# One load of a streaming add is issued in two parts, the second in short rows

## The chip, the cores and the metric

The kernel runs on one core of one Trainium2 chip. The metric is the device time of one execution in microseconds; the figure for a kernel is the median of its runs. A profile of one execution gives a span, from its first to its last instruction.

## The reference

```python
B, S, D = 512, 32, 640        # x, fx: bf16 [512, 32, 640]; alpha: bf16 [1]
def reference(x, fx, alpha):
    return x + alpha * fx
```

Each of the three large tensors holds 10,485,760 bf16 numbers, 20.97 MB. Two of them are read and one is written, so 62.91 MB pass through the core, with one multiplication and one addition for each number.

## The kernel before

The tensors are viewed as 128 partitions with 80 units in each. A unit is K = 1024 numbers, 2048 bytes, and the units of one partition lie next to each other in memory, so a piece of n units is 128 rows of n x 2048 bytes in a DMA.

`x` is cut into three pieces, X = units 0-32, 32-64 and 64-80, which are called x0, x1 and x2 here. `fx` is cut into five, FX = units 0-16, 16-32, 32-51, 51-67 and 67-80, called f0 to f4. The pools `wide` (for x) and `fs` (for fx) have two buffers each. So x2 takes the buffer of x0 and has to wait until the store of x0 has left it; f2 takes the buffer of f0 and waits for the computation on f0; f3 takes that of f1, and f4 that of f2.

The order is written out by hand in PLAN, which is carried out step by step; the scheduler moves nothing. In short:

```
x 0, a, f 0, f 1, x 1, c 0 0, f 2, c 1 0, s 0, f 3, x 2, c 2 1, f 4, c 3 1, c 3 2, s 1, c 4 2, s 2
```

- `x i` (load_x, line 77) and `f j` (load_f, line 85) load a piece, `s i` (store, line 104) stores one. All of them are DMAs that SP issues, in this order, on one hardware queue. x0 is issued as two DMAs, 4 units and 28 units (X_CUTS); every other piece is one DMA.
- `a` (alpha_to_lanes, line 109) loads alpha and spreads it over the 128 partitions with one small matmul; the result lands in `a_f`.
- `c j i` (compute, line 92) is one VectorE instruction, `x_t = f_t * a_f + x_t`, over the units that f_j and x_i share. It writes in place, and the store reads the x tile. f3 straddles x1 and x2 and has two of these (`c 3 1`, 13 units, and `c 3 2`, 3 units).

SP stands at an issue whose condition is not met yet, and everything behind it in the list waits too. Stores wait for VectorE, loads into a used buffer wait for VectorE or, for x2, for the store of x0. At the end SP waits for all that is under way (line 126).

Each DMA of 128 rows is spread over the core's 16 DMA engines, 8 rows to an engine: the trace holds 1730 packets, of which 1536 are rows (12 large DMAs x 128), and the rest are completions of 4 bytes and the one element of alpha. An engine works off its rows in the order of issue.

Of the kernel before, what the change touches and what calls it, by code (L numbers as in the profile page):

```python
# [2 lines left out]

# [4 lines left out]

ACT = mybir.ActivationFunctionType
ALU = mybir.AluOpType  # L10
F32 = mybir.dt.float32
BF16 = mybir.dt.bfloat16

K = 1024
P = 128


X = [(0, 32), (32, 64), (64, 80)]
FX = [(0, 16), (16, 32), (32, 51), (51, 67), (67, 80)]

X_CUTS = {0: (4,)}
PLAN = """
x 0
a
f 0
f 1
x 1
c 0 0
f 2
c 1 0  # L30
s 0
f 3
x 2
c 2 1
f 4
c 3 1
c 3 2
s 1
c 4 2
s 2  # L40
"""


@with_exitstack
def kernel(
    ctx: ExitStack,
    tc: tile.TileContext,
    x: bass.AP,
    fx: bass.AP,
    alpha: bass.AP,  # L50
    out: bass.AP,
):

    nc = tc.nc
    xv = x.flatten_outer_dims().rearrange("(p n) d -> p (n d)", p=P)
    fxv = fx.flatten_outer_dims().rearrange("(p n) d -> p (n d)", p=P)  # L60
    ov = out.flatten_outer_dims().rearrange("(p n) d -> p (n d)", p=P)
    assert xv.shape[1] == X[-1][1] * K == FX[-1][1] * K

    consts = ctx.enter_context(tc.tile_pool(name="consts", bufs=1))
    psum = ctx.enter_context(tc.tile_pool(name="psum", bufs=1, space=bass.MemoryType.PSUM))
    wide = ctx.enter_context(tc.tile_pool(name="wide", bufs=2))
    fs = ctx.enter_context(tc.tile_pool(name="fs", bufs=2))
    ctx.enter_context(tc.manual_schedule())

    xt, ft = {}, {}  # L70
    done = []

    def load_x(i):
        a, b = X[i]
        xt[i] = wide.tile([P, max(e - s for s, e in X) * K], x.dtype, tag="x", name="x_t")
        for c, d in pairwise((a, *X_CUTS.get(i, ()), b)):
            r = nc.sync.dma_start(  # L77
                out=xt[i][:, (c - a) * K : (d - a) * K], in_=xv[:, c * K : d * K]
            )
            done.append(r)  # L80

    def load_f(j):
        a, b = FX[j]
        ft[j] = fs.tile([P, max(e - s for s, e in FX) * K], fx.dtype, tag="f", name="f_t")
        r = nc.sync.dma_start(out=ft[j][:, : (b - a) * K], in_=fxv[:, a * K : b * K])
        done.append(r)

    def compute(j, i):
        (fa, fb), (xa, xb) = FX[j], X[i]
        a, b = max(fa, xa), min(fb, xb)  # L90
        piece = xt[i][:, (a - xa) * K : (b - xa) * K]
        r = nc.vector.scalar_tensor_tensor(  # L92
            out=piece,
            in0=ft[j][:, (a - fa) * K : (b - fa) * K],
            scalar=lanes["a_f"][:],
            in1=piece,
            op0=ALU.mult,
            op1=ALU.add,
        )
        done.append(r)  # L100

    def store(i):
        a, b = X[i]
        r = nc.sync.dma_start(out=ov[:, a * K : b * K], in_=xt[i][:, : (b - a) * K])
        done.append(r)

    lanes = {}

    def alpha_to_lanes():
        a_1 = consts.tile([1, 1], alpha.dtype, name="a_1")  # L110
        done.append(nc.sync.dma_start(out=a_1[:], in_=alpha[None, :]))  # L111
        ones = consts.tile([1, P], alpha.dtype, name="ones")
        nc.vector.memset(ones[:], 1.0)  # L113
        a_ps = psum.tile([P, 1], F32, name="a_ps")
        done.append(nc.tensor.matmul(a_ps[:], ones[:], a_1[:], start=True, stop=True))  # L115
        lanes["a_f"] = consts.tile([P, 1], F32, name="a_f")
        nc.vector.tensor_copy(out=lanes["a_f"][:], in_=a_ps[:])  # L117

    does = {"x": load_x, "f": load_f, "c": compute, "s": store, "a": alpha_to_lanes}
    for step in PLAN.split("\n"):  # L120
        if step:
            what, *of = step.split()
            does[what](*map(int, of))


    rest = nc.sync.nop(nofuse=True)
    info = mybir.DependencyInfo(mybir.DependencyClass.Sync, mybir.DependencyReason.DATA)
    for i in done[:-1]:
        tc.add_manual_dep(rest.ins, i.ins.name, info, reason="all but the last store")


# [1 line left out]
_INS = ['x', 'fx', 'alpha']  # L133
_OUTS = [((512, 32, 640), 'bfloat16')]


# [23 lines left out]
```

## Time and profile before

| | |
|---|---|
| median of 3 runs | 152.03 us (151.96 to 152.31) |
| span of the profiled execution | 150.2 us |
| median less span | 1.8 us |
| VectorE (DVE) busy | 86.8 us, 58% of the span |
| DMA queue: share of 16 engines | 98.1% |
| bytes moved | 62.92 MB, mean 419 GB/s |
| packets | 1730, of them 194 under 512 bytes |
| instructions | 78 |

The page times the profiled execution by its span alone; what lies ahead of the first instruction and behind the last one is not on it. The 1.8 us above are the difference between the median of the timed runs and that span, and they are taken as the same for both kernels.

Times are in microseconds from the start of the span. "DMA share" is the mean busy share of the 16 engines. In a window, a packet counts with all its bytes and its whole time in the window in which it starts; so a share can be above 1, and GB/s can be trusted only where the window's ends fall on the ends of rows. In the chain of waits, "DMA" is the time between the issue of a transfer and the moment its waiter is released.

### The profile page before, as it was taken

The numbers are of one execution on the slowest core, as the hardware profiler recorded it, in microseconds if no ns is written. First come the engines' busy times: TensorE is split into PE (matmuls) and PEld (weight loads), VectorE is DVE, ScalarE is ACT, GpSimd is POOL, SyncE is SP. The second block draws the span as 40 slices with busy tenths as digits, with TensorE's granted clock in tenths as the row PEclk, the third lists the DMA queues.
The fourth block names the chain that finished last, engine by engine and source line by source line (L and its number), as shares of the span: only waits on it lengthen the run. The fifth ranks groups of instructions, "written<-read, shape, count | busy, mean of one in ns | idle before, by whom it ended". The sixth has DMA issues, their size and how long they took to land.

```text
span 150.2 us, 78 instructions
## 1 busy us (share of the span) xinstructions
PE 0.2 (0%) x1; PEld 0.1 (0%) x1; DVE 86.8 (58%) x8; POOL 0.2 (0%) x4
## 2 busy tenths in 40 slices
PE   0000000000000000000000000000000000000000
PEld 0000000000000000000000000000000000000000
DVE  0000000049999999970399999106999999980000
POOL 0000000000000000000000000000000000000000
DMA  5997989999969696999696999999999969696994
GB/s 179 589 428 305 489 384 419 436 454 471 576 297 559 279 559 279 497 394 435 279 559 279 559 401 410 445 419 419 419 393 454 620 279 559 279 559 297 454 463 183
DMA packets 1730, 62.92 MB, mean 419 GB/s; under 512 B 194, under 2 KB 194, under 8 KB 194
## 3 DMA queue, kind: packets, MB, share of 16 engines
q1 hardware_dynamic: 1730, 62.92, 98.1%
HBM read 41.94 MB, written 20.97 MB: 419 GB/s over the span
## 4 chain that ended last, share of the span: by engine, by line
DMA 54%; DVE 35%; SPq 1%; issue 0%; DVEq 0%
DMA f_t<-in_fx_dram 54%; DVE x_t L92 35%; SPq L77 1%; SPq L111 0%; DVEq L92 0%
## 5 line engine op out<-in xcount | busy, mean ns | idle before, releaser
L92 DVE SCALAR_TENSOR_TENSOR x_t<-f_t,a_f,x_t 128x16384 bf16<-128x16384 bf16 (+3 forms) x6 | 86.5, 14438 | 25.5 <-DMA f_t<-in_fx_dram 25.5
L117 DVE COPY a_f<-a_ps 128x1 f32<-128x1 f32 x1 | 0.2, 159 | 21.5 <-PE a_ps L115 21.5
L113 DVE MEMSET ones<- 1x128 bf16 x1 | 0.2, 165 | 0.8 <-PEq L144 0.8
L115 PE MATMUL a_ps<-a,ones 1*128 1x1 bf16 x1 | 0.2, 158 | 22.2 <-DMA a<-in_alpha_dram 22.2
L144 POOL MEMSET const-bfloat16-1.0<- 128x1 bf16 x1 | 0.1, 103 | 0.0
L144 POOL MEMSET const-uint8-127<- 128x1 uint8 x1 | 0.1, 103 | 0.0
L115 PEld LDWEIGHTS <-ones 1*128 1x128 bf16 x1 | 0.1, 100 | 1.0 <-DVE ones L113 1.0
L144 POOL MEMSET const-float32-1.0<- 128x1 f32 x1 | 0.1, 100 | 0.0
L144 POOL MEMSET const-float32-0.0<- 128x1 f32 x1 | 0.1, 99 | 0.2 <-issue 0.2
## 6 DMA issues: line engine op xcount, KB each, us to landing
f_t<-in_fx_dram SPq DMA_DIRECT2D x3, 4096.0 KB, 35.6
x_t<-in_x_dram SPq DMA_DIRECT2D x1, 7168.0 KB, 21.3
f_t<-in_fx_dram SPq DMA_DIRECT2D x1, 4864.0 KB, 24.1
x_t<-in_x_dram SPq DMA_DIRECT2D x1, 4096.0 KB, 19.2
out_dram<-x_t SPq DMA_DIRECT2D x1, 4096.0 KB, 14.9
f_t<-in_fx_dram SPq DMA_DIRECT2D x1, 3328.0 KB
x_t<-in_x_dram SPq DMA_DIRECT2D x1, 1024.0 KB, 4.8
out_dram<-x_t SPq DMA_DIRECT2D x2, 24.7
```

The costliest lines, as they stand in the source:

```text
L77: r = nc.sync.dma_start(out=xt[i][:, (c - a) * K : (d - a) * K], in_=xv[:, c * K : d * K])
L92: r = nc.vector.scalar_tensor_tensor(out=piece, in0=ft[j][:, (a - fa) * K : (b - fa) * K], scalar=lanes["a_f"][:], in1=piece, op0=ALU.mult ...
L113: nc.vector.memset(ones[:], 1.0)
L115: done.append(nc.tensor.matmul(a_ps[:], ones[:], a_1[:], start=True, stop=True))
L117: nc.vector.tensor_copy(out=lanes["a_f"][:], in_=a_ps[:])
L144: nc = _bacc.Bacc("TRN2", target_bir_lowering=False, num_devices=1)
```

## The change

The third fx piece, f2 (units 32 to 51), is loaded by two DMAs rather than one. The first takes units 32 to 49, 17 units, in one row of 34,816 bytes per partition as before. The second takes units 49 to 51 and is issued with rows of at most 1024 bytes: each partition's 4096 bytes go as 4 rows, 512 rows in all, 32 to an engine. Both are issued on SP at the place of the old one. The instruction `c 2 1` waits for both.

The diff also brings in two other tables, S_CUTS and AFTER, which are empty: stores stay whole, no step gets another condition. The other DMAs keep their shapes.

```diff
+RUN = 1024
+F_CUTS = {2: (49,)}
+S_CUTS = {}
+AFTER = {}
...
     def load_f(j):
         a, b = FX[j]
         ft[j] = fs.tile([P, max(e - s for s, e in FX) * K], fx.dtype, tag="f", name="f_t")
-        r = nc.sync.dma_start(out=ft[j][:, : (b - a) * K], in_=fxv[:, a * K : b * K])
-        done.append(r)
+        for c, d in pairwise((a, *F_CUTS.get(j, ()), b)):
+            r = nc.sync.dma_start(
+                out=ft[j][:, (c - a) * K : (d - a) * K],
+                in_=fxv[:, c * K : d * K],
+                max_dma_last_dim=RUN if c > a else 65536,
+            )
+            after(r, "f", j)
+            done.append(r)
+            parts["f", j, d] = r
...
     def store(i):
         a, b = X[i]
-        r = nc.sync.dma_start(out=ov[:, a * K : b * K], in_=xt[i][:, : (b - a) * K])
-        done.append(r)
+        for c, d in pairwise((a, *S_CUTS.get(i, ()), b)):
+            r = nc.sync.dma_start(
+                out=ov[:, c * K : d * K], in_=xt[i][:, (c - a) * K : (d - a) * K]
+            )
```

In the instruction lists of the two kernels SP has one row more, a DMA of 128x4x512 numbers behind one of 128x17408 where there was one of 128x19456. VectorE, TensorE and GpSimd have the same instructions in the same order.

## The prediction

> **What bounds the kernel.** I read the page first: which resource is full?
>
> ```profile
> PE 0.2 (0%) x1; PEld 0.1 (0%) x1; DVE 86.8 (58%) x8; POOL 0.2 (0%) x4
> ...
> q1 hardware_dynamic: 1730, 62.92, 98.1%
> ```
>
> VectorE works for 86.8 of 150.2 us; the DMA engines are busy for 98.1% of the span. So the end is set by 62.92 MB going through 16 engines, provided that the one queue never runs dry. The chain of waits names transfers and VectorE in turn, which could mislead, so I held SP's issues (the timeline) against the landings:
>
> ```profile
> 2.90 0.45 SPq L77 DMA_DIRECT2D x_t<-in_x_dram  x1
> 49.59 0.33 SPq L85 DMA_DIRECT2D f_t<-in_fx_dram  x1
> 66.78 0.35 SPq L104 DMA_DIRECT2D out_dram<-x_t  x1
> 67.19 0.42 SPq L85 DMA_DIRECT2D f_t<-in_fx_dram  x1
> 73.80 20.48 DVE L92 SCALAR_TENSOR_TENSOR x_t<-f_t,a_f,x_t 128x19456 bf16<-128x19456 bf16 x1 [7.04 <-DMA f_t<-in_fx_dram]
> 93.37 0.33 SPq L77 DMA_DIRECT2D x_t<-in_x_dram  x1
> 94.31 0.33 SPq L85 DMA_DIRECT2D f_t<-in_fx_dram  x1
> 116.95 17.96 SPq L104 DMA_DIRECT2D out_dram<-x_t  x2
> ```
>
> Every issue comes before the queue is empty. x1 lands 58.3 us after its issue at 2.90, at 61.2; f2 was issued at 49.59, 11.6 us ahead of that. f2 lands at 73.7; s0 and f3 were issued 6.9 and 6.5 us ahead. f3 lands at 102.8 (35.6 us after issue); x2 and f4 were there 9.4 and 8.5 us earlier. f4 lands at 120.4 and s1 was issued 3.5 us ahead; s2 was issued at 134.6, about 5 us ahead of the end of s1. VectorE's waits are therefore waits for the same queue, and the whole kernel moves as one with the time that the engines take per row.
>
> So the question is where the engines run below their pace. With windows whose ends fall on row ends (columns: window, its length, the engines' busy times, clock, DMA share, GB/s):
>
> ```profile
> 60.20:68.84 8.64, 0.00 (x0) 0.00 (x0) 6.56 (x1) 0.00 (x0) 1.00 1.00 432
> 68.84:72.98 4.14, 0.00 (x0) 0.00 (x0) 0.00 (x0) 0.00 (x0) 1.00 1.00 301
> 72.98:92.30 19.32, 0.00 (x0) 0.00 (x0) 18.50 (x1) 0.00 (x0) 1.00 1.00 434
> 111.65:119.54 7.89, 0.00 (x0) 0.00 (x0) 7.89 (x2) 0.00 (x0) 1.00 1.00 432
> ```
>
> The first two are f2: six rows of each engine at 432 GB/s, then the last two at 301. The third is s0, at 434 at once. The fourth is the whole of f4, which also has a store behind it, at 432 to its end. The DMA view of the slow window says the same by packets: 32 packets, two for each engine, and the engines are never free in it.
>
> ```profile
> DMA packets 32, 1.25 MB, mean 301 GB/s; under 512 B 0, under 2 KB 0, under 8 KB 0
> ...
> q1 hardware_dynamic: 32, 1.25, 100.4%
> ```
>
> The packet records of the trace put sizes to it. A row of 38,912 bytes takes 1439 to 1448 ns in rows 1 to 6 of f2, about 1.6 us in row 7 and about 2.5 us in row 8, on all 16 engines; the excess is 1.28 us per engine. Outside of f2 only the first rows of the kernel show one (0.5 us, the 8192-byte rows at the start, 392 to 876 ns where 309 is usual). The slow rows are the ones at which s0 (issued 66.78) already stands behind f2; the change puts short rows exactly there.
>
> **What the change costs.** Rows first. Usual durations by size are 309 ns (8192 B), 987 (26,624), 1213 (32,768), 1439 (38,912), 2116 (57,344) and 2418 (65,536): a straight line of 36.78 ns per 1000 bytes plus 7.7 ns, and each row starts 3 ns before the last one ends, so a row costs 4.7 ns beyond its bytes. An engine's 8 long rows lose 4096 bytes each, and 32 rows of 1024 bytes come in: 32 x 4.7 = 0.15 us, and one more completion packet of 9 ns, overlapped by 3. Sum **+0.16 us** on every engine, on the path. No large row here is below 8192 bytes, so 4.7 ns is the line continued; below, a row cannot cost less than nothing (0 us), and above I bound it by the excess that the 8192-byte rows had in their slow start, 83 ns at least: 32 x 83 = 2.7 us. I take the line, since six sizes lie on it and the start has ended by 3.3 us.
>
> The other edits. SP issues one more DMA, 0.3 to 0.5 us by its other issues, at 49.9; its next step is s0 at 66.78, held by VectorE, so 16 us cover it, and without that cover s0 would still be 6 us early. The queue gets one more completion; `c 2 1` waits for one more semaphore, a few hundredths by the chain's own steps (0.02 to 0.05 us), and what is behind it, f4's issue at 94.3, is 8.5 us early. These go at nothing.
>
> One rule speaks against the cut; this row comes first: four DMAs stand behind one another between 2 and 61 us, and x1 of 65,536-byte rows follows f1 without a gap. The Trainium skill ("DMA: Bandwidth & Descriptors", Anatomy of one DMA, and Rules for kernel authors) gives each DMA about 2.0 us fixed, measured on the GpSimd path, and asks for 1 MiB or more; the new part has 0.5 MB. By that the sum would be 2 us worse, 154.0. The trace shows back-to-back DMAs of this queue at 432 to 434 GB/s, so I leave it at zero.
>
> **What the change may bring.** Most to gain is the 1.28 us. The engine that was last when x1 ended (row end at 60.78) lost 1.1 us of it and is last at f2's end too (73.41); the last engine counts, so without the slow stretch f2 lands about **1.1 us** earlier. With +0.16 that is -0.98. What the slow stretch depends on is not in the trace. Two readings:
>
> Reading by rows: an engine takes up the next rows in its list before the current one is through, and when those belong to a store, the load's rows share the engine with it. Row 7 (0.2) and row 8 (1.07) are the two before s0. If it looks ahead by a few rows, few short rows are hit, a few kilobytes rather than 50. For it: the loss begins when the store is two rows off, and load behind load has none. f4 escaping fits if s1 (issued 116.95, some 2.6 us ahead of the first s1 row at 119.55) came too late to be taken up beside f4's rows. Reading by bytes: the stretch is the last 50 KB or so (row 8 and a third of row 7), whatever the rows are. Then nothing is won.
>
> A row that bears on this: f4's slowest engine ends its last row at 119.99 and the load is seen to have landed at 120.44, 0.45 us; at 27.2 bytes per ns, 12 KB are under way. Against it the Trainium skill ("HBM Reference", Latency) has 2 us for an access under high load; an estimate from that page is 54 KB under way, close to the stretch, which would speak for bytes and for a time of 152.2. I go with the row: 12 KB under way do not explain 50 slow KB, so it is not a matter of bytes alone.
>
> I take the reading by rows as the likeliest and let a fifth of a microsecond of the stretch remain (as row 7 kept 0.2 of it when the store was one row further off): -1.1 + 0.2 + 0.16 = -0.77, taken as -0.8 us. Span 150.2 - 0.8 = 149.4; with the 1.8 us around it, 152.03 - 0.8 = **151.2 us**. After f2 everything moves forward together: `c 2 1` starts at about 73.0, x2 and f4 are issued 0.8 earlier, s1 at about 116.1, 3.5 us ahead of f4's landing as before. Next late is still the queue.
>
> **The rivals.** (1) The stretch stays as long as it was: by bytes, or tied to the time since s0's issue, or an accident of this one execution that the median doesn't hold. Then only the rows count: 152.03 + 0.16 = 152.2 us. For it: one profile; f4 with no loss shows that a store behind a load is not enough. Against it: all 16 engines have it, and only there.
> (2) Slower: in the stretch the delay is paid per row, and there are 32 rows in place of one. For it: the start of the kernel, where 8192-byte rows, the shortest here, lost 83 to 567 ns each, while the 57,344-byte rows after them lost almost none. Against it: the start's rows recover within 2 us, with the same sizes. The balance lies where 32 short rows lose what the stretch lost less the 0.16: (1.28 - 0.16) / 32 = 35 ns per row, a row of 77 ns in place of 42. At 60 ns per row it is 1.9 + 0.16 - 1.28 = +0.8, 152.8 us; at 83 ns +1.5, 153.6.
> (3) The change does not do what it says: the rows might be joined again into long ones. The instruction list shows 128x4x512, so I give it no chance of its own; it would give 152.0.
>
> **How the numbers follow.** Forecast (stretch mostly gone, 150.9 to 151.6) 0.45; rival 1 (152.0 to 152.5) 0.27; rival 2 (152.4 to 153.6) 0.28. A measurement of this kernel can tell about 0.2%, 0.3 us, from no change. Rival 1 lies within that in 0.20 of its 0.27 and above it in 0.07. Faster 0.45, same 0.20, slower 0.07 + 0.28 = 0.35. The range must hold 8 in 10: from 150.9, all of the stretch gone with the row costs at zero, up through rival 1 and a third of rival 2, to 152.7. The forecast's own range is 150.9 to 151.6.
>
> **What would show it.** Right: the packets are 1730 + 512 rows + 16 = 2258; f2 lands near 72.9, the window of its last rows is above 400 GB/s, and short rows take 42 to 50 ns. s0 runs at 434 again. Wrong, by rival 1: f2 lands at 73.8, and the slow part now holds the short rows and the last long row, together still 1.2 us too long. Wrong, by rival 2: short rows above 77 ns and f2 landing after 74. Wrong in the ground: a gap in the queue in front of s0 or s1, or VectorE waiting for something else than the queue.

## The result and the profile after

The changed kernel took 152.30 us (median of 20 runs, 152.02 to 152.75) against 152.07 us for the kernel before (20 runs). The ratio is 1.0015, 95% interval 1.0009 to 1.0021: 0.23 us slower (0.14 to 0.32). The prediction was 151.2 us and faster; the figure of its first rival was 152.2. In a later comparison (e15 below) the same kernel stood at 0.9998 (0.9988 to 1.0008), no difference. So the change brought nothing; the 0.23 us were not seen a second time.

The lines of the page (span 150.4 us) that answer to those of before:

```profile
PE 0.2 (0%) x1; PEld 0.1 (0%) x1; DVE 86.8 (58%) x8; POOL 0.2 (0%) x4
...
q1 hardware_dynamic: 2258, 62.92, 98.0%
```

The packets are the 2258 of the prediction, and the kernel is bound as before. SP's issues and VectorE's wait for f2, from the timeline:

```profile
49.38 0.81 SPq L97 DMA_DIRECT2D f_t<-in_fx_dram  x2
66.57 0.35 SPq L123 DMA_DIRECT2D out_dram<-x_t  x1
66.97 0.43 SPq L97 DMA_DIRECT2D f_t<-in_fx_dram  x1
74.05 20.48 DVE L110 SCALAR_TENSOR_TENSOR x_t<-f_t,a_f,x_t 128x19456 bf16<-128x19456 bf16 x1 [7.51 <-DMA f_t<-in_fx_dram]
```

`c 2 1` starts at 74.05, where 73.0 was forecast and 73.80 was measured before. f2 did not come earlier. The windows show why; a row counts in the window in which it starts. The first has the first seven long rows of each engine and five of the sixteen eighth ones, the second the other eleven and 409 of the 512 short rows, the third the rest of the short rows and s0:

```profile
60.18:69.33 9.15, 0.00 (x0) 0.00 (x0) 6.36 (x1) 0.00 (x0) 1.00 1.05 445
69.33:73.00 3.67, 0.00 (x0) 0.00 (x0) 0.00 (x0) 0.00 (x0) 1.00 0.81 218
73.00:92.30 19.30, 0.00 (x0) 0.00 (x0) 18.25 (x1) 0.00 (x0) 1.00 1.02 440
```

At the usual pace one long row (1285 ns) and 32 short ones (42.4 ns) take 2.64 us. By the packet records an engine needed 3.90 us on average from the start of its eighth long row to the start of its first row of s0. The slow stretch is still there, in the same 3 to 4 us ahead of s0. The packet records show its make: of the 512 short rows 425 took 48 ns or less, 81 took more than 60, up to 451. So the short rows are not all slowed alike: most go at their usual pace, some are held up.

Below, "excess" is the time per engine that f2's rows (of whatever length) took beyond the line of the prediction, 36.78 ns per 1000 bytes plus 7.7 ns; it comes from the packet records of each run's one profile. It was 1.30 us before and 1.13 us after. Where rows are short it counts too little, because the engines also stand between two rows. From the first row of f2 to the first row of s0, on average over the engines, the load took 12.79 us before and 12.92 us after; that is 1.29 and 1.27 us beyond the usual pace of the rows. So the stretch lost as much as before, and the 0.13 us between the two loads is nearly the price of the short rows.

### The profile page after: what moved, and what is told of

Its sections match the earlier page's. It is cut to its first block, busy times and chain, and to the rows that moved or that the text cites. A ratio compares the mean times of both kernels' runs of the same rounds, so it can differ in the third digit from the quotient of the medians.

```text
span 150.4 us, 80 instructions
## 1 busy us (share of the span) xinstructions
PE 0.2 (0%) x1; PEld 0.1 (0%) x1; DVE 86.8 (58%) x8; POOL 0.2 (0%) x4
## 2 busy tenths in 40 slices
DMA packets 2258, 62.92 MB, mean 418 GB/s; under 512 B 210, under 2 KB 722, under 8 KB 722
## 3 DMA queue, kind: packets, MB, share of 16 engines
q1 hardware_dynamic: 2258, 62.92, 98.0%
## 4 chain that ended last, share of the span: by engine, by line
DMA 53%; DVE 34%; SPq 1%; issue 0%; DVEq 0%
DMA f_t<-in_fx_dram 53%; DVE x_t L110 34%; SPq L88 1%; SPq L97 0%; SPq L135 0%; DVEq L110 0%
```

## Experiments

All ratios are to the kernel before, on the same chip. All edits are made to the changed kernel's code, whose tables stand at `RUN = 1024`, `F_CUTS = {2: (49,)}`, `AFTER = {}`; AFTER names a DMA that is issued only when another has landed. The edits are shown in short. A letter such as R or S is a theory that the expectation of the run names.

**The cut without the short rows** (e1).

```diff
-RUN = 1024
+RUN = 65536
```

> f2 is cut at unit 49 as in the changed kernel, but the second part keeps long rows (128 rows of 4096 bytes, 8 to an engine). Theory S (a store that already stands in the queue slows the last 3 us or so of the load in front of it, whatever its rows are): the stretch stays at about 1.1 to 1.3 us per engine, and only 8 rows of 4.7 ns and one completion come in: +0.05 us on the kernel before, 152.1. Theory P (the loss belongs to the place or the moment, f2's own last bytes): the same. Theory R (the added time of the changed kernel comes from the split and the second semaphore, not from the short rows): 152.3, as the changed kernel.

151.86 us, ratio 0.9996 (0.9987 to 1.0006), excess 0.79 us. One more DMA, one more semaphore and 8 rows of 4096 bytes per engine cost nothing that can be measured. R, by which the cut itself costs the time, falls.

**The store moved behind f3** (e2).

```diff
-F_CUTS = {2: (49,)}
+F_CUTS = {}
-f 2, c 1 0, s 0, f 3, x 2, c 2 1, f 4, c 3 1
+f 2, c 1 0, f 3, s 0, c 2 1, f 4, x 2, c 3 1
```

> The kernel before with f3 issued ahead of s0, and f4 ahead of x2, so that f2 is followed by a load and f3 by the store; s1 is issued as soon as c 3 1 is done, which is some 10 us before x2 has landed. Theory S: f2's last rows go at 1439 to 1448 ns, the last 2 rows of f3 lose 1.1 to 1.3 us per engine instead, and x2's last rows lose as much again, because s1 now stands behind x2 long ahead: two stretches, about 153.2 us. Theory P: f2's last two rows lose 1.28 us as before and f3 and x2 lose nothing, 152.1.

152.04 us, 0.9999 (0.9988 to 1.0009). Windows: all of f2, then f3's first six rows per engine, then its last two, which are in front of s0 now.

```profile
60.40:71.93 11.53, 0.00 (x0) 0.00 (x0) 6.40 (x1) 0.00 (x0) 1.00 1.01 435
71.93:79.15 7.22, 0.00 (x0) 0.00 (x0) 6.27 (x1) 0.00 (x0) 1.00 1.00 431
79.15:82.30 3.15, 0.00 (x0) 0.00 (x0) 3.15 (x1) 0.00 (x0) 1.00 1.01 333
```

The stretch went with the store: f2 is clean (longest row 1449 ns), f3's end is slow, by 0.77 us. VectorE works all through it here and was idle in it before, so it has no part in it. P, by which the loss belongs to f2's own last bytes, falls. But S had a second stretch in front of s1, and there was none: x2's rows had no excess, although s1 was issued 12 us before they ended.

**s0 later, in three steps** (e3, e16 and e9).

```diff
-RUN = 1024
+RUN = 65536
-F_CUTS = {2: (49,)}
+F_CUTS = {2: (45,)}                      # e16: 42, e9: 46
-AFTER = {}
+AFTER = {("s", 0): ("f", 2, 45)}         # e16: 42, e9: 46
```

> f2 is cut at unit 45 with long rows in both parts, and s0 is issued only when the first part has landed, some 3 us before the second part has. Theory S: the store is not there yet while the engines take up f2's last bytes, as it is with s1 behind f4, and the loss is gone: f2's rows all at the pace of 36.78 ns per 1000 bytes, about 1.1 us less the row costs, 151.0 us. Theory P: f2's end loses 1.1 to 1.3 us all the same, 152.1. If s0 comes too late, a gap of some tenths shows ahead of its first row.

> f2 cut at unit 42 with long rows, s0 issued when the first part has landed, some 5.5 us before f2's end, between the 4.1 us (loss 0.37) and the 6.9 us (0.8 to 1.3) already seen. If the loss grows with the time that the store has stood in the queue: 0.5 to 0.9 us per engine, time 0 to 0.2 us under the kernel before. If there is a step at a fixed lead of 3 to 4 us, the full 0.8 to 1.3 us. If any wait of s0 for a part of f2 helps, whatever the lead: 0.1 us or less, 151.5.

> As the run in which s0 waits for the first part of f2, but cut at unit 46, so that s0 is issued some 3 us before f2's end rather than 4; s1 behind f4, with 3.5 us and no loss, lies between. If the loss depends on how long the store has stood in the queue: f2's rows lose 0.0 to 0.2 us per engine where that run had 0.34 and the kernel before 1.28, and the time is 0.5 to 0.9 us under the kernel before, 151.1 to 151.5. If that run's smaller loss was chance: 0.3 to 1.3 us again, 151.5 to 152.0.

| s0 issued ahead of f2's landing | excess at f2 | us | ratio |
|---|---|---|---|
| 6.2 us (e16) | 0.81 us | 151.98 | 0.9997 (0.9987 to 1.0006) |
| 4.1 us (e3) | 0.38 us | 151.67 | 0.9978 (0.9968 to 0.9989) |
| 3.0 us (e9) | 0.06 us | 151.53 | 0.9965 (0.9952 to 0.9977) |

The issue of s0 and the start of `c 2 1`, just after f2's landing, in e16 and then in e9:

```profile
67.56 0.35 SPq L123 DMA_DIRECT2D out_dram<-x_t  x1
73.85 20.48 DVE L110 SCALAR_TENSOR_TENSOR x_t<-f_t,a_f,x_t 128x19456 bf16<-128x19456 bf16 x1 [6.95 <-DMA f_t<-in_fx_dram]
```

```profile
69.94 0.35 SPq L123 DMA_DIRECT2D out_dram<-x_t  x1
73.08 20.48 DVE L110 SCALAR_TENSOR_TENSOR x_t<-f_t,a_f,x_t 128x19456 bf16<-128x19456 bf16 x1 [6.20 <-DMA f_t<-in_fx_dram]
```

The windows of e9, f2's first eight rows per engine, its second part, and s0:

```profile
60.25:68.78 8.53, 0.00 (x0) 0.00 (x0) 6.63 (x1) 0.00 (x0) 1.00 1.00 430
68.78:71.87 3.09, 0.00 (x0) 0.00 (x0) 0.00 (x0) 0.00 (x0) 1.00 0.95 398
71.87:91.20 19.33, 0.00 (x0) 0.00 (x0) 18.12 (x1) 0.00 (x0) 1.00 1.02 438
```

The second window ends with the first start of s0, so the last rows of the engines behind count in the third; the row records are sharper: none of e9's 10,240-byte rows took more than 396 ns, where the line gives 384. No gap stands ahead of s0. This version is faster than the kernel before by 0.53 us (0.35 to 0.73), and a store that comes late enough leaves the load alone. Not all of the loss is won: s0's own last rows, in front of f3, lost 0.16 us per engine in e9 and 0.13 us in e3, where they lost nothing in the kernel before and in e16.

**f3 issued late** (e4) and **s0 issued when f2 has landed** (e12).

```diff
-F_CUTS = {2: (49,)}
+F_CUTS = {}
+AFTER = {("f", 3): ("f", 2, 51)}         # e12: ("s", 0): ("f", 2, 51)
```

> The kernel before, only that f3 is issued when f2 has landed, so that s0 stands alone behind f2. Theory F (what slows f2's end is the load behind the store, which the engines take up at the same time): the loss is gone, 151.0. Theories S and P: f2's last two rows lose 1.1 to 1.3 us as before, 152.1; f3 is then still issued 19 us ahead of its turn.

> s0 is issued only when f2 has landed, so that nothing stands behind f2. If it takes a store in the queue to make the loss: f2's rows are clean, f2 lands at about 72.5; then the queue is empty until s0's first row, by the start of the kernel about 1.0 us from issue to first row plus 0.45 us of landing, so 151.97 - 0.9 + 1.5 = 152.6. If the loss is there without any store behind: 153.5.

e4: 151.92 us, 0.9996 (0.9987 to 1.0005), excess 0.81: a load behind the store is not what does it; F, which said so, falls. e12: 153.90 us, 1.0124 (1.0110 to 1.0138), excess 0.03; f2's last two rows:

```profile
69.00:71.95 2.95, 0.00 (x0) 0.00 (x0) 0.00 (x0) 0.00 (x0) 1.00 0.98 422
```

With no store in the queue there is no stretch. The time is 1.3 us above what was expected: the engines stood 1.7 us on average between f2's rows and s0's (from 73.85), and another 0.77 us went where it was not looked for, in s0's own last rows from 90.8 us on (up to 3533 ns where 2418 is usual), in front of f3. f4's end lost 0.2. A store in front of a load can be slowed too.

**Which store** (e5, e7, e11, e8).

```diff
 # all four: f2 uncut
-F_CUTS = {2: (49,)}
+F_CUTS = {}
 # e5, e7: unit 0 of x0 stored by itself right after c 0 0; in e7 on ScalarE's queue
+S_CUTS = {0: (1,)}
+c 0 0, s 0 (first part), f 2, c 1 0, s 0 (rest), f 3
 # e11: units 0 to 2 stored right behind f2
+S_CUTS = {0: (2,)}
 # e8: all of s0 on ScalarE's queue
+r = nc.scalar.dma_start(...)
```

> The kernel before, with unit 0 of x0 stored by a DMA of its own (128 rows of 2048 bytes) as soon as c 0 0 is done, ahead of f2, and the other 31 units at the old place. Theory W (the first store of an execution slows the load in front of it, whichever store that is): the loss moves to the last rows of x1, which is now in front of the first store, at 0.8 to 1.3 us per engine; f2's rows are clean; the time stays within 0.1 us of the kernel before. Theory Z (the loss belongs to the store of x0's 64-KB rows): x1's rows are clean and f2's last two rows lose 0.8 to 1.3 us as before.

> As the run with the small first store of unit 0, but this store is issued on ScalarE's queue, so that the loads on SP's queue do not stand behind or in front of it. Theory W, where the loss is a wait inside one queue: it is paid beside the loads, f2's last rows are clean, x1's too, 151.1. Theory W, where the loss falls on whatever the engines carry at that moment: some rows of x1 lose 0.8 to 1.3 us at about 50 to 53 us, f2's are clean, 152.0. Theory Z: f2's last two rows lose as before, 152.0.

> s0 is cut at unit 2: its first two units (128 rows of 4096 bytes) are issued right behind f2, 23 us before f2's end, and the other 30 at the old time. If the loss grows with the time that a store has stood behind the load: f2's end loses at least as much as in the kernel before, 0.8 to 1.3 us or more, 152.0. If it depends on the size of the store's rows that the engines have next (64 KB in the kernel before, 4 KB here): f2's end loses a few tenths at most, 151.2 to 151.5.

> The kernel before with s0 issued on ScalarE's queue: its rows alternate with the loads from about 68 us on, and no load stands in front of it in its queue. A wait inside one queue (W or Z): no rows lose, 151.1, if SP's queue never runs dry (f2 lands later, at about 80, c 2 1 ends at about 100, f4 is issued then, while f3 and s0 still run). A loss that falls on whatever the engines carry: rows near 69 to 72 us lose 0.8 to 1.3 us, 152.0.

e5: 151.75 us, 0.9984 (0.9975 to 0.9994); x1's last row lost 0.17 us and f2 still 0.54: the loss did not move from f2 to the load in front of the first store, so W, by which the first store does it, falls as it was put. Z expected 0.8 to 1.3 us at f2 and nothing at x1, and does not fit this run either. e7: 151.94 us, 0.9995 (0.9986 to 1.0004); excess at f2 1.08 us although a store had run before, and x1's rows lost nothing. e11: 151.89 us, 0.9995 (0.9986 to 1.0004), about 0.7 us at f2 with rows of 4096 bytes behind it and 23 us of lead: small rows in the store did not take it away, and more lead did not raise it. e8: 154.75 us, 1.0186 (1.0164 to 1.0207): rows lost time where the two queues ran beside each other (0.8 us at 69) and in front of s1 (1.0 us at 119 to 122), and the engines stood all but still around 102 to 103.5, because x2 and f4 were issued only at 102.7 and 103.1, after s0 had landed, when f3 was all but through.

**The price of the rows** (e6, e10, e17, e18, e13).

```diff
-F_CUTS = {2: (49,)}
+F_CUTS = {1: (24,)}     # e6: 128 short rows per engine in f1
+F_CUTS = {1: (30,)}     # e10: 32 in f1; e17: the same cut, RUN = 65536
+F_CUTS = {0: (14,)}     # e18: 32 in f0
+F_CUTS = {2: (46, 49)}  # e13: short rows from 49 on; AFTER = {("s", 0): ("f", 2, 46)}
```

> f2 is whole again; instead the second half of f1 (units 24 to 32, 16,384 bytes per partition) goes in rows of 1024 bytes, 128 to an engine, with no store anywhere near. By the line through the row durations of the kernel before, 4.7 ns for each row: 0.60 us, 152.0 + 0.6 = 152.5. By the rate at which the changed kernel lost against the kernel before (0.23 us for 32 rows, 7.2 ns each, were the slow stretch the same in both): 0.92 us, 152.9. If the short rows cost nothing away from a store: 152.0.

> The same 512 short rows of 1024 bytes, 32 to an engine, as in the changed kernel, but as the end of f1 (units 30 to 32), where a load follows. Row price: the 128 short rows of the earlier run took 46 to 60 ns, 9.3 ns on average beyond their bytes; 32 of these are 0.30 us, or 0.15 us by the line of the large rows. If the short rows alone make the changed kernel slower, this one is 0.15 to 0.30 us slower too, 152.15 to 152.3, and f2's end keeps its loss of 0.8 to 1.3 us. If short rows anywhere ahead of f2 shift the engines against each other so that the loss goes (as it had gone in the run with 128 of them): f2 clean, 0.5 to 0.9 us faster, 151.2 to 151.5.

> f1 cut at unit 30 with long rows in both parts, the control for the run with 32 short rows per engine at the same place, which was 0.23 us faster with 0.29 us lost at f2's end. If the short rows did that (by shifting the engines against each other ahead of f2), this run has the usual 0.7 to 1.3 us at f2's end and the time of the kernel before, 152.0. If the cut, or one more DMA in the queue, did it: 0.3 us at f2's end, 151.75.

> The same 512 short rows as the end of f0 (units 14 to 16), another place with no store near. If short rows ahead of f2 lessen the loss at its end: 0 to 0.4 us there, row price 0.15 to 0.3 us, time 0.1 to 0.4 us under the kernel before. If the run with f1 was chance: 0.7 to 1.3 us at f2's end, and the row price is all that is left, 152.15 to 152.3.

> f2 in three parts: units 32 to 46 and 46 to 49 in long rows, 49 to 51 in the changed kernel's 512 short rows; s0 is issued when the first part has landed, some 3 us before f2's end. The price of the short rows without the slow stretch: if it is what the other runs show (46 to 50 ns a row, 0.15 to 0.25 us in all, with 8 rows and one completion more for the third part, 0.05 us), the time is 0.2 to 0.3 us above the run with the cut at 46 alone, that is 0.2 to 0.3 us below the kernel before. If short rows cost more when a store follows, it is at or above the kernel before. If the late store doesn't take the loss away here, waits of 90 to 450 ns show between the short rows again.

| run | short rows | mean ns of one | excess at f2 | us | ratio |
|---|---|---|---|---|---|
| e6 | 128 in f1 | 50.1 | 0.03 us | 152.46 | 1.0030 (1.0019 to 1.0041) |
| e10 | 32 in f1 | 47.3 | 0.31 us | 151.77 | 0.9985 (0.9976 to 0.9993) |
| e17 | none, cut in f1 | - | 0.75 us | 151.91 | 0.9998 (0.9989 to 1.0007) |
| e18 | 32 in f0 | 46.2 | 0.29 us | 151.71 | 0.9984 (0.9975 to 0.9993) |
| e13 | 32 in f2, late s0 | 48.8 | 0.13 us | 151.44 | 0.9964 (0.9951 to 0.9976) |

A row of 1024 bytes takes 46.2 to 50.1 ns, less the 3 ns of overlap, and 37.7 ns are its bytes: 32 of them are 0.18 to 0.30 us. In e13 no short row took more than 60 ns; so short rows by themselves don't bring the long waits of the changed kernel on. In e6, uncut in f2, some 1.2 us of row price (128 x 9.4 ns) stand against a stretch that is gone, and 0.46 us are left. That e13 is as fast as e9, and not 0.2 us slower as was expected, is within the two intervals.

The same 32 short rows, in f0 or f1, made the kernel 0.24 and 0.23 us faster, while the cut alone (e17) did nothing. The windows of f2's last two rows, e17 first and e18 second:

```profile
69.00:72.63 3.63, 0.00 (x0) 0.00 (x0) 0.00 (x0) 0.00 (x0) 1.00 0.99 343
```

```profile
69.30:72.47 3.17, 0.00 (x0) 0.00 (x0) 0.00 (x0) 0.00 (x0) 1.00 0.99 393
```

In these profiles f2's stretch is smaller with short rows ahead of it, by more than the rows cost, and the times agree. I had thought of the distance of the 16 engines from each other: the first rows of f2 start within 0.56 us before, 0.36 in e10, 0.41 in e18. But it is 0.25 in e3 with 0.38 us of excess, and 0.44 in e6 with 0.03. By itself it does not order the runs.

**Both kernels once more** (e14, the uncut kernel; e15, the changed one).

> The kernel before with the new code and empty tables: the same instructions, for a second profile of the stretch. If the 1.28 us of the first profile are the rule, they are here again; if each execution draws its own loss, this one lies anywhere in 0.3 to 1.3 us, as in the runs in which f2's end was left as it was (0.77 to 1.08).

> The changed kernel once more, for a second profile of the short rows. If the rows leave the stretch as it is: 0.3 to 1.3 us of excess, in few rows, most of them at 46 ns. If the first profile was an unlucky one and short rows do take the loss away: under 0.3 us.

e14: 151.92 us, 0.9998 (0.9988 to 1.0008), excess 0.82. e15: 151.96 us, 0.9998 (0.9988 to 1.0008), excess 0.57 including the short rows' own, 51 of 512 above 60 ns. With the time between rows, as above, f2 took 12.31 us in e14 and 12.40 us in e15, 0.81 and 0.76 us beyond the usual pace of the rows. f2's end, uncut in e14 and with the short rows in e15:

```profile
69.00:72.68 3.68, 0.00 (x0) 0.00 (x0) 0.00 (x0) 0.00 (x0) 1.00 1.00 338
```

```profile
69.50:72.81 3.31, 0.00 (x0) 0.00 (x0) 0.00 (x0) 0.00 (x0) 1.00 0.85 276
```

The stretch differs from profile to profile. With s0 6 to 7 us ahead and f2 uncut the profiles gave 1.30, 0.82, 0.81 and 0.75 us of excess (before, e14, e4, e17); with the short rows, and the time between rows counted, 1.27 and 0.76. Each is one execution, and e4, e14 and e17 ran on three chips, so whether the size changes with the execution or with the chip is not shown.

## Why the prediction was wrong

- **What bounds the kernel:** right. Where the queue stayed filled, the span is the time of an engine's rows, less their overlaps, plus 3.1 to 3.6 us. That holds to a few tenths, not to the hundredth.
- **The row price, +0.16 us:** right in kind and nearly in size. The line gave 45.4 ns; most rows took 46, the means away from a stretch were 46.2 to 50.1, so 0.18 to 0.30 us. The Trainium skill ("Advanced Engine Details and Errata", Clock Domains) has 42 to 43 ns for an unobstructed descriptor of 1 KiB, which agrees with most rows here, 46 ns less 3 ns of overlap.
- **The second DMA at nothing:** right (e1, -0.06 us, -0.20 to +0.09). The fixed cost of about 2.0 us that the Trainium skill ("DMA: Bandwidth & Descriptors", Anatomy of one DMA) measured on the GpSimd path does not show here for a DMA that stands in SP's filled queue.
- **-1.1 + 0.2 us for the stretch:** this is the step that failed. It rested on the reading by rows, that an engine looks a few rows ahead. With 32 rows of 1 KB in it the stretch lost 1.27 and 0.76 us, against 0.75 to 1.30 with f2 uncut, and f2 took 0.13 and 0.10 us longer than in the uncut kernel (after against before, e15 against e14) where 0.7 to 0.8 us less was forecast. Rows of 4096 bytes in the store behind did not help either (e11). So short rows at the end of the load don't shrink it. I had ruled the other reading out by 12 KB under way against 50 slow KB; that argument counted the landing of one load, and it was no evidence about the stretch. The 2 us at high load that the Trainium skill ("HBM Reference", Latency) has for an access, by the prediction's estimate 54 KB under way at 27.2 bytes per ns, spoke against the change. That is close to the 50 KB or so of the stretch; no run here measures such a latency, so it is not shown as the cause.
- **The size of the prize:** mis-sized as well. 1.28 us (1.30 by the line) was the largest of four profiles, 0.92 us on average; with the stretch all but gone the kernel gains 0.53 us (e9) and 0.55 (e13), not the 0.98 us of the sum, also because s0's end loses a little then. Two small slips in the working: -0.98 and -0.77 go by 1.14 us, the terms as they are written give -0.94 and -0.74; and 83 ns is not the least that a row of the slow start lost, since one of the first 16 took 315 ns. Neither turns the forecast.
- **f4 escapes because s1 came late:** borne out for s0, in three steps of lead (0.81, 0.38, 0.06 us). It is not the whole of it: in e2 s1 was issued 12 us before x2's end, and x2 lost nothing.
- **Rival 1** had the mechanism and nearly the time: the stretch as long as it was, and the rows on top. **Rival 2**, a price per row in the stretch, does not hold: most rows in it run at their usual 46 ns, the mean was 66 ns (59 in e15) and not above 77, and the load as a whole lost no more than with long rows.

Settled: the slow end of f2 needs the store in the queue early (e2, e12, and the three leads), it is not VectorE, not f3, not the place in fx, and short rows inside it don't remove it. Open: what in the engines or the memory it is, why s1 did not bring it on in e2, and why f2 lost less with short rows in f0 or f1. So the cause of the stretch itself stays open. The first comparison (+0.23 us) and the second (-0.03) are of the same two kernels, and the row price is the same in both; that the stretch differed is likely and not shown.

## What to carry to other kernels

A slow place in a trace shows that something is slow there; what it depends on must be tried before an edit is priced by it, and its size should be read from several executions. Where a full queue of loads has a store behind it, look at the last 3 to 4 us of the load: issuing the store about 3 us before the load ends, by making it wait for an early part of that load, was worth 0.35% in this kernel and needed no short rows. Issued only after the load had landed, the same store cost 1.24% (e12). Rows of 1024 bytes cost 6 to 9 ns each beyond their bytes. That is little, but where they win nothing it is all that is left.

## What the hardware showed beyond that

- A DMA of many short rows can hold the issuing queue. In e6 (2048 rows, 128 per engine) SP came to the next issue, x1, at 3.56 us and was through with it only at 37.1, when the short rows had begun to run (36.3 us); with 32 per engine (e10) the same issue took 0.55 us. The first two lines are e6, the third is e10.

```profile
1.99 1.53 SPq L97 DMA_DIRECT2D f_t<-in_fx_dram  x3
3.56 33.58 SPq L88 DMA_DIRECT2D x_t<-in_x_dram  x1
```

```profile
3.47 0.55 SPq L88 DMA_DIRECT2D x_t<-in_x_dram  x1
```

Nothing waited for SP in those 33 us here. SP's issues go in the order of the list, so a store or a buffer's reload that stood behind such an issue would wait; no run shows that case.
